# A routing phase that starts from the marked logits instead of from its predecessor's token indices

## The chip, the cores and the metric

The kernel runs on one core of one Trainium2 chip. The metric is the device time of one execution in microseconds (us). The core has five engines that work side by side: TensorE (PE, with its weight loads shown apart as PEld), VectorE (DVE), ScalarE (ACT), GpSimd (POOL) and SyncE (SP), which here only issues transfers. Each takes its instructions strictly in the order in which the program lists them.

## What is computed

Three layers follow one another (shapes: batch 8, 8 heads, 576 positions, 64 channels, so 4608 tokens of 512 channels; 8 experts with a hidden width of 1024; a last hidden width of 2048):

```python
x = linear_attention(q, k, v)
logits = x @ w_gate
order = argsort(-logits.flatten())
for idx in order:
    tok, e = idx // 8, idx % 8
    if assigned[tok] >= 0 or counts[e] >= 576: continue
    assigned[tok] = e; counts[e] += 1
for e in range(8):
    mask = assigned == e
    out[mask] = relu(x[mask] @ w1[e]) @ w2[e]
h = out @ w_in
return (h * clip(h + 3, 0, 6) / 6) @ w_out
```

The greedy assignment gives every expert exactly 576 tokens. Whichever expert fills up first can be settled without the others, and its tokens with it; what is left is the same problem with one expert fewer.

## The kernel before

**Routing.** `phase(ph)` (from L804) settles one expert. It takes the largest logit of each token (`m`, L808), marks which expert it belongs to (`eq`, `oh`), and finds the cut of each expert by eight rounds of counting (`counts`, `digit`): one comparison on VectorE (`ge`, L766), a product on TensorE (L777), two small VectorE steps with another product between them (`blk` L780, L785, `cnt` L788), then `hit` (L795) and one more product (L798) whose result the next round needs. So a round goes back and forth between the two engines three times. The expert that fills up first is `ei` (L889); its tokens are marked in `sel` (L874). From `sel` two things follow. One is the list of token indices: five MAX (L896) and four match-and-replace steps (L901), a comparison of 640 columns (`ind`, L894 and L898), ten small products (L911), three steps on `eq5`, and at last `gi` (L920). The other is that the settled expert and tokens are struck out of the logits `L` (L927, L928), from which the next phase reads.

**Experts.** `gather(ph)` fetches the 576 tokens in five tiles by an indirect transfer from POOL (`xg`, L1000), scales them on VectorE (L1006), transposes them on TensorE (L1019, four blocks a tile) and splits each result into a high part on ScalarE (L1024) and a low part on VectorE (L1029), both in `xT`, of which there is one buffer. `expert(ph)` does two halves of 288 tokens. Each half has 96 products with w1 (L1049, called A here) and 96 with w2 (L1071, called B); the eight results of A in each half are `h` (L1053, L1058). `xT` is free again after A of the second half. `load_expert(ph)` reads `ei` and loads 16 weight chunks of 256 KB (`st`, L980 and L983), each of which ScalarE (L497) and VectorE (L954) split into two parts.

**What sets the order.** The program lists its operations with their inputs and outputs, and a planner (`Sched`) places them by a list schedule: each engine takes, in planned time, the ready operation of highest priority. Routing phases after the first have a priority just above that of the expert products. The planned order of each engine is then the program's order. So routing phase ph + 1 stands between the products of expert ph, on TensorE and on VectorE, and what an edit does to a dependency shows as another order of all engines.

The calls at the end stand like this, and the first phase has nothing of an expert beside it, only the end of the attention layer:

```python
phase(0); gather(0); load_expert(0)
for ph in range(E):
    if ph + 1 < E: phase(ph + 1)
    expert(ph)
    if ph + 1 < E: load_expert(ph + 1); gather(ph + 1)
```

After the experts, the last layer (L1231, L1259) takes more than half of the time. Its weights are converted (`conv`, L1079 and on) from the time on at which the gather of phase 6 is done.

Of the kernel before, what the change touches and what calls it, by code (L numbers as in the profile page):

```python
# [15 lines left out]
OP = mybir.AluOpType  # L16
AX = mybir.AxisListType
# [29 lines left out]
class Sched:  # L47
# [17 lines left out]
    def op(self, eng, dur, fn, r=(), w=(), prio=0, lat=None, pen=None, u=()):  # L65
        i = len(self.ops)
        deps = set()
        for n in r:
            deps.update(self.writers.get(n, ()))
            self.readers.setdefault(n, []).append(i)  # L70
        for n in w:
            if any(x != i for x in self.readers.get(n, ())):
                deps.update(x for x in self.readers[n] if x != i)
                self.writers[n] = []
                self.readers[n] = [i] if n in r else []
            if n in self.bufof and n not in self.first:
                self.first[n] = i
                deps.update(self.writers.get(("pool", self.bufof[n][3]), ()))
            self.writers.setdefault(n, []).append(i)
        for n in set(r) | set(w) | set(u):  # L80
            if n in self.bufof:
                self.users.setdefault(n, []).append(i)
        if isinstance(eng, str):
            eng = [(eng, dur)]
        self.ops.append((eng, fn, deps, prio + self.base, lat, pen or dict(PENALTY)))
        return i
# [127 lines left out]
def tile_attn_moe_mlp(ctx, tc, q, k, v, w_gate, w1, w2, w_in, w_out, out):  # L214
    nc = tc.nc
    V, S, P, T, Y = nc.vector, nc.scalar, nc.gpsimd, nc.tensor, nc.sync
# [14 lines left out]
    def dve(n, x=1, ps=False):  # L231
        return ((130 if ps else 64) + n / x) / 0.96
# [12 lines left out]
    op = sc.op  # L245
# [24 lines left out]
    def const(name, shape, dt=F32):  # L270
        return (main if name in ("idxf", "idx", "spacer", "three") else PL["route"][1]).tile(shape, dt, name=name)
# [44 lines left out]
    L = const("L", [128, NCOL, E])  # L316
# [372 lines left out]
    m = const("m", [128, NCOL])  # L689
# [45 lines left out]
    n288 = NCOL * E  # L735
# [4 lines left out]
    def vop(n, f, r, w, x=1):  # L740
        op("dve", dve(n, x), f, r=r, w=w, prio=prio[0], lat=None if prio[0] == -1 else SLACK.get(w[0]))
# [62 lines left out]
    def phase(ph):  # L804
        odd = ph % 2
        last = ph == E - 1
        gate = [("gi", ph - 1)] if ph else []
        vop(n288, lambda e: V.tensor_reduce(m, L, axis=AX.X, op=OP.max), ["L"] + gate, ["m"])  # L808
        if not last:
            vop(n288, lambda e: V.tensor_tensor(eq, L, per_c(m), op=OP.is_equal), ["L", "m"], ["eq"])  # L810
            vop(NCOL, lambda e: V.tensor_scalar(ks, m.bitcast(I32), 31, 0x7FFFFFFF, op0=OP.arith_shift_right,
# [321 lines left out]

    prio[0] = -1
    phase(0)
    prio[0] = RPR
    gather(0)
    load_expert(0)
    for ph in range(E):
        if ph + 1 < E:  # L1140
            phase(ph + 1)
        expert(ph)
        if ph + 1 < E:
            load_expert(ph + 1)
            gather(ph + 1)
# [191 lines left out]
```

## Time and profile before

| | |
|---|---|
| median of 3 runs | 1499.53 us (1495.55 to 1502.17) |
| the profiled execution | 1508.03 us, its span 1505.6 us |
| PE busy | 1412.7 us, 94% |
| PEld, DVE, ACT, POOL busy | 1229.8, 673.0, 444.0, 600.4 us |
| mean granted clock of PE | 0.971 of full speed |

The profiled execution is 8.5 us above the median; differences are worked out inside it and then taken off the median. "PE busy" counts any time in which a product is under way, whatever the clock is, so a stretch can be fully busy and yet do less than another. The clock column gives the mean of the granted TensorE clock as a share of 2.4 GHz; its other level is 1.2 GHz, so 0.75 over a stretch is half of it at each.

### The profile page before, as it was taken

What the parts mean: (1) busy time and instruction counts of PE and PEld (TensorE: products, weight loads), DVE (VectorE), ACT (ScalarE), POOL (GpSimd) and SP (SyncE); (2) the same over time, 40 slices, a digit from 0 to 9 for tenths busy, and PEclk for the clock granted to TensorE, in tenths of its full rate; (3) what the DMA queues carried; (4) which work ended last, traced back from release to release, by engine and by line L of the source; (5) the groups of instructions that cost most, each with busy time, mean ns of one, the idle gap of its engine ahead of it and who ended that gap; (6) DMA issues with size and microseconds to landing.
All of it is one profiled execution on the core that took longest, in us unless ns stands there. A gap on an engine that the chain in (4) does not pass through costs nothing.

```text
span 1505.6 us, 23079 instructions
## 1 busy us (share of the span) xinstructions
PE 1412.7 (94%) x8738; PEld 1229.8 (82%) x8738; DVE 673.0 (45%) x1646; ACT 444.0 (29%) x858; POOL 600.4 (40%) x752
## 2 busy tenths in 40 slices
PE   5889599989999998899999999999999999999997
PEld 4778598989889898799788888888888888888886
DVE  7996668676675867875761111111111111111110
ACT  3656334233242434454432121211212121121111
POOL 6784301010110105755675353543535353353433
PEclk9999788999999999999999999999999999999999
DMA  9683535133250438767411010100101010010000
GB/s 317 206 251 112 185 104 164 59 117 103 82 172 32 150 92 264 221 217 252 134 61 57 1 56 1 43 14 1 57 0 56 1 51 6 0 43 0 29 1 28
DMA packets 130559, 140.76 MB, mean 93 GB/s; under 512 B 21264, under 2 KB 104208, under 8 KB 130448
## 3 DMA queue, kind: packets, MB, share of 16 engines
q1 hardware_dynamic: 124496, 119.73, 25.4%
q0 software_dynamic: 5952, 19.56, 3.7%
q8 instruction: 68, 1.11, 0.3%
q14 instruction: 43, 0.35, 0.1%
HBM read 104.51 MB, written 34.75 MB: 92 GB/s over the span
## 4 chain that ended last, share of the span: by engine, by line
PE 70%; DVE 12%; DMA 9%; issue 3%; POOL 3%; ACT 2%; SPq 0%; POOLq 0%; DVEq 0%; ACTq 0%
PE acc L1259 24%; PE mm L1231 23%; PE mm L1071 8%; PE mm L1049 8%; DMA st<-in_moe_w_dram 5%; PE px L619 2%; DMA wh<-co 2%; DVE m L384 1%; PE pkv L520 1%; DVE wq L954 1%; DVE xg L1006 1%; POOL out_dram L1277 1%; PE tr L1019 1%; DMA cs<-in_moe_w_in_dram 1%; DMA ys<-yd 1%
## 5 line engine op out<-in xcount | busy, mean ns | idle before, releaser
L1237 DVE SCALAR_TENSOR_TENSOR t<-t,mm 128x512 f32<-128x512 f32 x144 | 98.8, 687 | 540.2 <-ACT t L1236 530.6
L1236 ACT ACTIVATE t<-mm,three 128x512 f32<-128x512 f32 x144 | 99.1, 689 | 557.8 <-PE mm L1231 544.4
L501 POOL TENSOR_SCALAR G<-t 128x512 fp32r<-128x512 f32 x124 | 78.2, 631 | 365.7 <-DVE t L1237 362.6
L1259 PE MATMUL acc<-wq,G 128*128 128x512 f32 x864 | 211.9, 393 | 3.5 <-ACT G L497 1.6
L1231 PE MATMUL mm<-yT,wq 128*128 128x512 f32 x864 | 207.2, 389 | 0.0
L1259 PEld LDWEIGHTS acc<-wq,G 128*128 128x128 f32 x864 | 162.4, 189 | 41.7 <-POOL G L954 5.3
L1231 PEld LDWEIGHTS mm<-yT,wq 128*128 128x128 f32 x864 | 162.1, 188 | 33.6
L1000 POOL DMA_INDIRECT xg<-xd,gi x40 | 46.8, 1171 | 352.8 <-issue 307.1
L954 POOL TENSOR_TENSOR G<-t,G 128x512 fp32r<-128x512 f32 x139 | 179.4, 1291 | 12.1 <-ACT G L497 1.6
L1071 PE MATMUL mm<-h,wq 128*128 128x288 f32 x960 | 143.9, 306 | 0.0
L1049 PE MATMUL mm<-xT,wq 128*128 128x288 f32 x960 | 141.4, 304 | 0.0
L1071 PEld LDWEIGHTS mm<-h,wq 128*128 128x128 f32 x960 | 134.7, 195 | 2.4 <-issue 2.4
L1049 PEld LDWEIGHTS mm<-xT,wq 128*128 128x128 f32 x960 | 132.8, 192 | 0.8 <-DVE h L1058 0.3
L1231 PE MATMUL mm<-yT,w 128*128 128x512 f32 x432 | 103.4, 389 | 0.0
L1231 PEld LDWEIGHTS mm<-yT,w 128*128 128x128 f32 x432 | 81.1, 188 | 16.8
L1259 PE MATMUL acc<-w,G 128*128 128x512 f32 x384 | 92.3, 389 | 0.0
L1259 PEld LDWEIGHTS acc<-w,G 128*128 128x128 f32 x384 | 72.0, 188 | 15.1 <-POOL G L954 0.2
L1053 ACT ACTIVATE h<-mm 128x288 fp32r<-128x288 f32 x128 | 51.1, 405 | 84.5 <-PE mm L1049 46.9
L1058 DVE SCALAR_TENSOR_TENSOR h<-mm,h 128x288 fp32r<-128x288 f32 x128 | 57.4, 450 | 15.7 <-ACT h L1053 15.0
L497 ACT ACTIVATE wq<-st 128x512 fp32r<-128x512 f32 x78 | 48.9, 630 | 43.7 <-DMA st<-in_moe_w_dram 43.1
L1117 POOL TENSOR_TENSOR ca<-ct,cl 128x256 int32<-128x256 int32 x64 | 50.1, 787 | 27.2 <-DVE ct L1113 18.4
L954 DVE TENSOR_TENSOR wq<-st,wq 128x512 fp32r<-128x512 f32 x76 | 51.9, 685 | 14.4 <-ACT wq L497 13.4
(241 smaller groups left out, 2193.5 us busy)
## 6 DMA issues: line engine op xcount, KB each, us to landing
st<-in_moe_w_dram SPq DMA_DIRECT2D x124, 256.0 KB
yd<-yo SPq DMA_DIRECT2D x64, 144.0 KB
xd<-xs SPq DMA_DIRECT2D x32, 260.0 KB
lk<-in_k_dram SPq DMA_DIRECT2D x16, 512.0 KB
wu<-in_v_dram SPq DMA_DIRECT2D x16, 512.0 KB
wl<-in_q_dram SPq DMA_DIRECT2D x16, 512.0 KB
cs<-in_moe_w_in_dram SPq DMA_DIRECT2D x32, 256.0 KB
cs<-in_moe_w_out_dram SPq DMA_DIRECT2D x32, 256.0 KB
```

The costliest lines, as they stand in the source:

```text
L497: S.activation(o, i, AF.Copy)
L501: P.tensor_scalar(o, i, 1.0, 0.0, op0=OP.mult, op1=OP.add)
L954: EN[e].tensor_tensor(t[:, 1], view(X[src]), t[:, 0].bitcast(F32), op=OP.subtract)
L1049: T.matmul(p[:, :HC], w[:, a, k_], X[XT][:, b_, k_, o:o + HC], start=(k_ == 0 and (a, b_) == (0, 0)), stop=(k_ == 3 and (a, b_) == (1, 0)))
L1053: op("act", act(HC), lambda e, pk=pk, hn=hn: S.activation(hn()[:, 0], X[pk][:, :HC], AF.Relu), r=[pk], w=[hk, (hk, 0)])
L1058: V.scalar_tensor_tensor(t[:, 1], X[pk][:, :HC], 0.0, t[:, 0].bitcast(F32), op0=OP.max, op1=OP.subtract)
L1071: T.matmul(p[:, :HC], w[:, a, 128 * d:128 * d + 128], h[:, b_], start=(f_ == 0 and (a, b_) == (0, 0)), stop=(f_ == NFE - 1 and (a, b_) == ...
L1117: op("pool", pool(256), lambda e: P.tensor_tensor(X[A].bitcast(I32), X[T_], X[L_], op=OP.add), r=[T_, L_, A], w=[A], prio=CVP)
L1231: T.matmul(p, w[:, a, d], X[YT][:, b_, d], start=(d == 0 and (a, b_) == (0, 0)), stop=(d == 3 and (a, b_) == (1, 0)))
L1236: op("act", act(512), lambda e: S.activation(tn(), X[pk], AF.Relu, bias=three), r=[pk], w=[tk])
L1237: op("dve", dve(512, ps=True), lambda e: V.scalar_tensor_tensor(X[tk], X[tk], 6.0, X[pk], op0=OP.min, op1=OP.mult), r=[pk, tk], w=[tk])
L1259: T.matmul(p, g[:, a, 128 * t:128 * t + 128], w[:, b_], start=(f_ == 0 and (a, b_) == (0, 0)), stop=(f_ == NFM - 1 and (a, b_) == (1, 0)))
```

## The change

`phase(ph)` for ph > 0 no longer names `gi` of phase ph - 1 as an input of its first operation. The logits `L`, with the last expert and its tokens struck out, remain its input.

```diff
     def phase(ph):
         odd = ph % 2
         last = ph == E - 1
-        gate = [("gi", ph - 1)] if ph else []
-        vop(n288, lambda e: V.tensor_reduce(m, L, axis=AX.X, op=OP.max), ["L"] + gate, ["m"])
+        vop(n288, lambda e: V.tensor_reduce(m, L, axis=AX.X, op=OP.max), ["L"], ["m"])
```

One line is gone, so line numbers from L808 on are one lower in the changed program. The arithmetic is the same; the planner orders all of it anew. Two places show it.

VectorE, where phase 0 ends and phase 1 begins. `idw`, `gi` and `idxf` are the end of phase 0's indices, `m`, `eq`, `ks` the start of phase 1. Before:

```order
L918 TENSOR_REDUCE idw<-eq_236 128x5
L920 TENSOR_SCALAR gi<-idw 128x5
L922 TENSOR_TENSOR idxf<-idxf,idw 128x5
L808 TENSOR_REDUCE m<-L 128x36
L810 TENSOR_TENSOR eq<-L,m 128x288
L811 TENSOR_SCALAR ks<-m 128x36
L813 TENSOR_TENSOR eq<-eq,wfirst 128x288
```

With the change, right after the second MAX of phase 0:

```order
L807 TENSOR_REDUCE m<-L 128x36
L897 SCALAR_TENSOR_TENSOR ind<-iota,off_230,ind 128x640
L900 MATCH_REPLACE score<-ids,score 128x36
L809 TENSOR_TENSOR eq<-L,m 128x288
L895 MAX ids<-score 128x8
L810 TENSOR_SCALAR ks<-m 128x36
```

and where `gi` of phase 0 now stands:

```order
L914 TENSOR_TENSOR eq_236<-iota,kk 128x200
L780 TENSOR_TENSOR blk<-rt,colm 128x64
L916 TENSOR_TENSOR eq_236<-eq_236,rt 128x200
L917 TENSOR_REDUCE idw<-eq_236 128x5
L919 TENSOR_SCALAR gi<-idw 128x5
L921 TENSOR_TENSOR idxf<-idxf,idw 128x5
```

Twelve instructions of phase 1, from `m` to the `blk` of its first round, now stand ahead of `gi` of phase 0, between its steps.

TensorE, where expert 0 ends and expert 1 begins: `tr` is a transpose of gathered tokens, `mm<-h` is B of expert 0, `mm<-xT` is A of expert 1, `rt` belongs to routing. Before, the first transposes stand behind the last of B:

```order
L1071 MATMUL mm<-h,wq 128x288 x12
L785 LDWEIGHTS samen
L785 MATMUL rt<-blk,samen 128x64
L1071 MATMUL mm<-h,wq 128x288 x6
L798 LDWEIGHTS ones_110
L798 MATMUL rt<-sat,ones_110 128x1
L1019 MATMUL tr<-ident,xg 128x64 x4
```

and, after five products L777 of a routing round, the rest of them just ahead of A:

```order
L777 MATMUL rt<-oh,ge 128x64
L1019 MATMUL tr<-ident,xg 128x128 x12
L785 LDWEIGHTS samen
L785 MATMUL rt<-blk,samen 128x64
L1049 MATMUL mm<-xT,wq 128x288 x6
```

With the change the first transposes stand 36 products ahead of the end of B:

```order
L1070 MATMUL mm<-h,wq 128x288 x12
L1018 MATMUL tr<-ident,xg 128x64 x4
L785 LDWEIGHTS samen
L785 MATMUL rt<-blk,samen 128x64
L1070 MATMUL mm<-h,wq 128x288 x6
L1018 MATMUL tr<-ident,xg 128x128 x4
```

and B and A meet without a transpose between them:

```order
L777 LDWEIGHTS ge
L777 MATMUL rt<-oh,ge 128x64
L1070 MATMUL mm<-h,wq 128x288 x6
L1048 MATMUL mm<-xT,wq 128x288 x6
L785 LDWEIGHTS samen
L785 MATMUL rt<-blk,samen 128x64
```

At each of the later boundaries the transposes have likewise moved from the last dozen of B, or from behind it, into B or ahead of it. Counted in the 16 steps `h` that each expert has on VectorE, `gi` of phases 1 to 6 stood behind `h` number 16, 32, 47, 64, 80 and 95, and stands behind number 14, 27, 40, 56, 72 and 88; `ei` stood behind 10, 24, 40, 56, 72 and 88 and stands behind 8, 24, 40, 54, 68 and 82. The order of the products of the last layer is the same.

## Rows read from the trace of the kernel before

**Rows 1.** The page: busy tenths and granted clock of PE, 40 slices.
```profile
PE   5889599989999998899999999999999999999997
...
PEclk9999788999999999999999999999999999999999
```

**Rows 2.** Stretches: length, busy PE, PEld, DVE, ACT, POOL, granted clock, DMA share, GB/s.
```profile
245.00:265.00 20.00, 16.52 (x104) 14.43 (x103) 14.06 (x35) 6.70 (x14) 3.08 (x3) 0.74 0.40 139
300.00:330.00 30.00, 24.46 (x180) 23.19 (x179) 21.95 (x57) 12.04 (x23) 5.14 (x5) 0.89 0.50 155
368.00:394.00 26.00, 22.27 (x176) 20.62 (x176) 21.67 (x58) 11.32 (x22) 7.08 (x5) 1.00 0.60 185
432.00:456.00 24.00, 20.42 (x153) 18.77 (x153) 19.97 (x53) 11.63 (x23) 6.09 (x5) 0.94 0.60 189
500.00:528.00 28.00, 24.87 (x190) 23.20 (x189) 21.49 (x57) 11.35 (x23) 6.76 (x5) 0.94 0.40 127
557.00:586.00 29.00, 22.34 (x167) 21.16 (x166) 25.83 (x69) 14.75 (x29) 11.09 (x10) 0.94 0.77 235
262.00:300.00 38.00, 38.00 (x310) 36.49 (x308) 23.31 (x95) 9.69 (x22) 0.00 (x0) 1.00 0.17 53
394.00:432.00 38.00, 38.00 (x310) 36.56 (x309) 23.88 (x95) 9.71 (x23) 0.00 (x0) 1.00 0.18 56
```

**Rows 3.** Waits of PE, 240 to 586 us: total us, times, longest us.
```profile
PE rt L785 <- DVE blk L780: 8.3, 5, 3.8
PE tr L1019 <- DVE xT L1029: 4.4, 4, 2.3
PE rt L911 <- DVE ids L903: 3.7, 3, 2.0
PE rt L911 <- DVE ids L904: 2.6, 5, 1.2
PE tr L1019 <- DVE xg L1006: 2.4, 5, 0.7
```

**Rows 4.** Waits of PE, 586 to 705 us.
```profile
PE tr L1019 <- DVE xT L1029: 3.9, 1, 3.9
PE tr L1019 <- issue: 3.5, 2, 2.3
```

**Rows 5.** Timeline of DVE, end of phase 0: start us, us, line, operation.
```profile
173.49 0.19 DVE L896 MAX8 ids<-score 128x8 f32<-128x36 f32 x1
...
179.70 0.32 DVE L920 TENSOR_SCALAR gi<-idw 128x5 int32<-128x5 f32 x1
...
180.01 0.44 DVE L808 TENSOR_REDUCE m<-L 128x36 f32<-128x288 f32 x1
...
182.64 0.76 DVE L766 SCALAR_TENSOR_TENSOR ge<-ra,iota 128x576 bf16<-128x576 f32 x1
183.95 0.23 DVE L780 TENSOR_TENSOR blk<-rt,colm 128x64 f16<-128x64 f32 x1 [0.54 <-PE rt L777]
```

**Rows 6.** The same at the end of phase 1.
```profile
231.23 0.19 DVE L896 MAX8 ids<-score 128x8 f32<-128x36 f32 x1
...
240.50 0.17 DVE L920 TENSOR_SCALAR gi<-idw 128x5 int32<-128x5 f32 x1
...
240.65 0.44 DVE L808 TENSOR_REDUCE m<-L 128x36 f32<-128x288 f32 x1
```

**Rows 7.** Line L920, 440 to 500 us: durations in ns, first and last start.
```profile
L920 DVE TENSOR_SCALAR gi<-idw x1: 158/158/158, 499.7 to 499.7; 128x5 int32<-128x5 f32 x1
```

**Rows 8.** Timelines of ACT, DVE, PE: one wait for weights, passed on.
```profile
315.64 0.63 ACT L497 ACTIVATE wq<-st 128x512 fp32r<-128x512 f32 x1 [4.20 <-DMA st<-in_moe_w_dram]
...
316.30 0.69 DVE L954 TENSOR_TENSOR wq<-st,wq 128x512 fp32r<-128x512 f32 x1 [3.60 <-ACT wq L497]
...
317.18 0.21 PE L785 MATMUL rt<-blk,samen 128*128 128x64 f16 x1 [3.83 <-DVE blk L780]
```

**Rows 9.** Timeline of PE: a group of four transposes at full clock.
```profile
325.84 0.66 PE L1019 MATMUL tr<-ident,xg 128*128 128x128 f32 x4 [0.80 <-DVE xT L1029]
```

## The prediction

> **What bounds the kernel now.** I read the page's slices first [rows 1]. A slice is 37.6 us. From the 18th on (640 us, the last expert and the last layer) PE has a 9 in every slice, at full clock, so nothing is to be had there but from an earlier start. A 5, and clocks of 7 and 8, stand in slices 5 to 7, where the attention layer gives way to the experts; an 8 stands in slices 16 and 17, near the end of the experts; between them a 9 hides short stops. So the next view is the busy time in stretches [rows 2]: the first six hold one boundary between two experts each, the last two lie inside an expert. Inside, PE is busy for 38.00 of 38 us at full clock and does 310 products. At each boundary it is busy for less than the stretch, and the clock is lower in five of the six. The two undisturbed stretches give 76 us / 620 = 0.1226 us a product, with routing among them. The six boundary stretches last 157 us together and hold 970 products, which at that rate are 118.9 us. About 100 of these are transposes (20 for each expert, some of the first stand ahead of the stretch or behind it); a group of four takes 0.66 us [rows 9], 0.165 each, which adds some 4.2 us. So **33.9 us** of the 157 are lost. PE is idle for 157 - 130.9 = 26.1 us of them; the other 7.8 us I put down to products at the lower clock.
>
> What it waits for stands in the list of waits [rows 3]. The transposes and the ten products of the index list wait for DVE; the largest entry, 8.3 us, is a routing product waiting for `blk`, and behind that is another thing: ScalarE waited 4.20 us for a weight chunk, DVE stood 3.60 us behind it, and PE 3.83 us behind `blk`, which is next in DVE's queue [rows 8].
>
> Why are the transposes late? Because the indices are. Phase by phase `gi` comes at 179.70 [rows 5], then 240.50 [rows 6], and that of phase 5 at 499.7 [rows 7]: (499.7 - 179.7) / 5 = 64.0 us a phase. The next phase's `m` starts 0.15 us behind `gi` at 240.65, though the logits were struck out before the second MAX at 231.23. PE's own work in that time, counted in the code: 384 products and 20 transposes of an expert, and 69 products of a routing phase (eight rounds of five L777 and one L785, seven L798, and 14 behind them). 473 x 0.1226 = 58.0 us, and the transposes' 20 x 0.042 on top make it 58.8. So the loop **routing, indices, next routing** (64.0) is longer than PE's work for an expert (58.8), and PE waits for the difference at each boundary.
>
> **The change, part by part.**
>
> *The wait that goes.* From phase 1 on, `m` can start after the second MAX: 240.65 - 231.23 = 9.4 us earlier against its own `gi`. The twelve instructions that now stand among the index steps put `gi` back. Their cost is read where they stand alone: from `m` at 180.01 to the end of the first `ge` at 182.64 + 0.76 = 183.40 is 3.4 us, and `blk` adds at most 0.23 [rows 5]. The new loop would be 64.0 - 9.4 + 3.4 = 58.0 us, just under PE's 58.8. So the routing loop stops being what is late, by a little, and **PE's own queue is late next**, with what else holds it up.
>
> *The first phase.* Here the same twelve instructions are pure loss, since PE and everyone else wait for `gi` of phase 0: nothing of an expert covers them. The lower bound is 0, if they fit into DVE's gaps; the only gap of size is the wait for the index products, about half a microsecond as in the `blk` row. The upper bound is 3.6. I take **+3.4 us**, the row itself. The gathers, the first multiplies and expert 0 follow by as much.
>
> *The boundaries.* The gathers, issued from POOL once `gi` is there, move ahead with it; POOL has nothing else to do in these stretches (0.00 busy in the undisturbed ones, [rows 2]), so they pass no other work on their queue. On TensorE the transposes now stand inside B, with products behind them that cover ScalarE's and DVE's splits. What PE loses to late indices and transposes should go; what it loses to `blk` behind the weights I leave in full, as the loads are the same ones, started by `ei`, which has moved by nothing to six steps. So of 26.1 us idle, 8.3 stay and **17.8 go**. Of the gather of the last phase, the 3.5 us for which two transposes were not yet there [rows 4] go too, as its `gi` now stands seven or eight steps earlier; the 3.9 us for `xT` I leave, since there DVE is behind with the conversion of the last layer's weights.
>
> *The clock.* At the first boundary the granted clock is 0.74 over 20 us [rows 2]: about 10 us at 1.2 GHz. At the third it is 1.00, with 3.7 us idle of 26, so stops don't always bring it down, nor would fewer stops bring all of it back. I let half of the 7.8 us return: **3.9**. The Trainium skill, "TensorE: Matmul & The Clock Gate", section "What's actually happening", has it that the low clock is the default and that activity lifts it; by that rule alone the whole 7.8 would return once the stops are gone, and the sum would be 3.9 us lower. The stretches agree with it in part: no stretch without a stop has a lower clock, and one with stops has none either.
>
> *SP's queue.* The reading of `ei` stands at the same place or a few stores earlier in it, with no new wait ahead. I cost it at nothing; the stores of expert results cover it, which nobody waits for until the last layer.
>
> *The last layer.* Its weights are converted after the gather of phase 6, and both move ahead together with the experts; its products stand in the same order. Nothing.
>
> Sum: 17.8 + 3.9 + 3.5 = 25.2 us gained, 3.4 lost, **21.8 us** less. From the profiled 1508.0 that is 1486.2; its execution is 8.5 us above the median, so from the median of 1499.5 I predict **1478 us**. Its own range: with 0 to 3.6 for the first phase, nothing or all of the clock, and a quarter of the 17.8 staying, 1470 to 1486.
>
> **The rivals.**
>
> *All of it goes.* With the routing ahead by more at each phase, the weights too are asked for earlier (`ei` moves by up to six steps), and the waits behind them vanish as well. Then 33.9 + 3.5 + 3.9 - 3.4 = 37.9 us less: **1462**. For it: the lead of `gi` grows from phase to phase, in the order, from 2 to 8 steps. Against: 58.0 and 58.8 are close, so on the chip that lead can be had only slowly.
>
> *The wait moves.* DVE remains as full: at the fourth boundary it is busy for 19.97 of 24 us [rows 2], and now two phases share its queue. If only the waits go that name the index list and the gathered tokens (3.7 + 2.6 + 2.4 = 8.7, [rows 3]), and the rest comes back as waits for `blk` and `h` inside B, the gain is 8.7 - 3.4 = 5.3: **1494**, no change that a measurement of this kernel can tell (about 0.5%, 7.5 us).
>
> *Slower: the gathers fall into the weight loads.* Before, `ei` starts 16 loads and the gathers come when a good part of these has landed. Now the gathers come a few steps behind `ei`. Each boundary could then have the stop of 3.83 us [rows 8] which so far one has in full: six of them are 23.0 instead of 8.3, 14.7 more. If half of the 17.8 then stays as well, because a DVE that waits for weights holds up `xT` too, the sum is +14.7 + 3.4 - 8.9 = +9.2: **1509**. It is slower by more than 7.5 us from the point at which the added stops exceed 7.5 - 3.4 + 8.9 = 13.0 us, 2.2 a boundary. For it: the chain through ScalarE, DVE and PE is there, and it began while gathers ran. Against: the loads are not needed so soon; A of the next expert comes a whole B later, and only the fixed order of the queues makes a late chunk hurt. The Trainium skill, "DMA: Bandwidth & Descriptors", section "Issuing engines are not separate DMA queues", says that transfers from SyncE and GpSimd run on the same 16 engines and interleave. That is the rule that speaks against this change; that a chunk was late just while gathers were out agrees with it, no more.
>
> **How the numbers follow.** Forecast 0.62, all of it 0.15, moved wait 0.14, slower 0.09. The two-loop sum, 58.0 against 58.8, carries the forecast; that the two are so close keeps its chance from being higher. The range takes in the forecast, the full gain with 5 us below it for the runs' own spread, and the moved wait up to a gain of nothing: 1457 to 1501. Faster by over 0.5% (below 1492): 0.62 + 0.15 = 0.77. Within 0.5%: 0.14. Slower: 0.09.
>
> **What would show it.** Right: `gi` of phase 0 near 183; a mean distance of `gi` of 58 to 61 us over phases 0 to 5; transposes that start without a wait, inside B; the list of waits without the index rows, with `blk` still there; clock 1.00 at most boundaries; expert 7 ending some 20 us earlier and the last layer as long as before. Wrong: a distance of `gi` still at 64 (the moved wait), or waits of ScalarE for weights grown at every boundary with `blk` behind them (slower), or no idle left at all (all of it).

## The result, and the profile after

The changed kernel takes 1486.94 us (1486.37 to 1487.82, 5 runs) beside 1502.17 us for the kernel before (1495.55 to 1503.77, 5 runs): a ratio of 0.9909, 95% interval 0.9886 to 0.9931. On another chip it was 1489.95 beside 1505.28, ratio 0.9902 (0.9882 to 0.9921). So some 15 us are gained. The profiled execution has a span of 1485.3 us, 20.3 less than before.

First the slices of the page of the changed kernel, against [rows 1]:

```profile
PE   5889689999999998899999999999999999999997
...
PEclk9999879999999999999999999999999999999999
```

The 8 of PE in slice 9, where expert 1 gives way to expert 2, is a 9 now, and from slice 7 on the clock has a 9 in every slice; the 8s in slices 16 and 17 have stayed. The larger view is the busy time in three long stretches: experts 0 to 5, experts 6 and 7, the last layer. Columns as in [rows 2]. The kernel before:

```profile
191.00:584.00 393.00, 366.53 (x2837) 347.39 (x2835) 277.11 (x909) 138.04 (x286) 41.48 (x34) 0.96 0.37 114
584.00:705.00 121.00, 112.28 (x799) 110.88 (x798) 87.89 (x172) 58.46 (x156) 78.90 (x107) 0.94 0.70 223
705.00:1505.00 800.00, 788.08 (x3454) 647.83 (x3452) 154.54 (x225) 152.86 (x260) 365.42 (x417) 1.00 0.10 35
```

The changed kernel:

```profile
197.00:565.00 368.00, 354.90 (x2843) 338.09 (x2842) 280.93 (x923) 141.70 (x303) 50.06 (x47) 0.99 0.43 133
565.00:683.00 118.00, 108.03 (x785) 105.23 (x784) 76.71 (x156) 53.36 (x145) 63.26 (x88) 0.99 0.68 219
683.00:1485.00 802.00, 787.86 (x3456) 646.95 (x3454) 154.16 (x229) 151.31 (x257) 360.28 (x416) 1.00 0.09 31
```

Three things stand in the first line of each. The stretch is 25.0 us shorter for nearly the same products (2837 and 2843). PE's idle time in it has halved, from 26.5 to 13.1 us. And PE's *busy* time has fallen by 11.6 us, because the mean clock rose from 0.96 to 0.99: fewer products run at 1.2 GHz. In the second line the idle time has not fallen (8.7 and 10.0 us). The busy time has, by 4.2 us: some 2 us of it are eleven transposes, which now stand ahead of the stretch, and most of the rest is clock (0.94 and 0.99). The last layer is the same within 2 us, and everything begins 6 us later.

The start of each expert, read from PE's timeline as its first product with `xT`, gives the account (us):

| | expert 0 | 1 | 2 | 3 | 4 | 5 | 6 | 7 | end of 7 | span |
|---|---|---|---|---|---|---|---|---|---|---|
| before | 191.1 | 257.7 | 326.4 | 390.7 | 454.0 | 518.1 | 584.0 | 652.6 | 704.5 | 1505.6 |
| changed | 197.5 | 263.1 | 322.9 | 384.5 | 442.9 | 503.8 | 564.6 | 628.5 | 682.9 | 1485.3 |

Start +6.4, six experts -25.8, experts 6 and 7 -2.2, last layer +1.3: -20.3. Of the +6.4, 1.8 lie ahead of anything that the change moves (`sel` of phase 0 starts at 173.6 instead of 171.8).

The loop that the prediction rests on, against [rows 5] and [rows 7]; line L919 is `gi`, of phase 0 and of phase 5:

```profile
L919 DVE TENSOR_SCALAR gi<-idw x1: 171/171/171, 185.7 to 185.7; 128x5 int32<-128x5 f32 x1
...
L919 DVE TENSOR_SCALAR gi<-idw x1: 158/158/158, 465.2 to 465.2; 128x5 int32<-128x5 f32 x1
```

(465.2 - 185.7) / 5 = 55.9 us a phase instead of 64.0, while the experts start (564.6 - 197.5) / 6 = 61.2 us apart instead of 65.5. So `gi` runs ahead: it comes 11.8 us before expert 0 starts and 38.6 us before expert 5 does (11.4 and 18.4 before). PE's timeline where expert 0 ends and expert 1 begins, with L1070 for B and L1048 for A:

```profile
255.69 0.46 PE L1018 MATMUL tr<-ident,xg 64*128 64x64 f32 x4
...
256.12 1.03 PE L1070 MATMUL mm<-h,wq 128*128 128x288 f32 x6
257.80 0.66 PE L1018 MATMUL tr<-ident,xg 128*128 128x128 f32 x4 [0.65 <-DVE xg L1005]
258.21 1.03 PE L1070 MATMUL mm<-h,wq 128*128 128x288 f32 x6
...
262.24 1.05 PE L1070 MATMUL mm<-h,wq 128*128 128x288 f32 x6
263.12 0.96 PE L1048 MATMUL mm<-xT,wq 128*128 128x288 f32 x6
```

The transposes stand among B, and A follows B without a stop. A group of four takes 0.66 us; the clock is 1.00 from 250 to 266 us. What PE still waits for from 197 to 565 us, against [rows 3]:

```profile
PE mm L1048 <- DVE h L1057: 3.4, 2, 1.9
PE rt L798 <- DVE hit L795: 2.7, 3, 1.3
PE tr L1018 <- issue: 2.2, 1, 2.2
PE rt L785 <- DVE blk L780: 1.5, 2, 1.2
PE tr L1018 <- DVE xg L1005: 1.4, 2, 0.7
PE rt L777 <- DVE ge L766: 1.0, 1, 1.0
PE tr L1018 <- DVE xT L1028: 0.5, 1, 0.5
PE rt L910 <- DVE ids L902: 0.2, 1, 0.2
```

The index list (`ids`) has gone from 6.3 to 0.2 us and `blk`, which I had left in full, from 8.3 to 1.5. The waits for `h` are new. Those for `hit` have grown; the kernel before had this row from 191 to 584 us:

```profile
PE rt L798 <- DVE hit L795: 1.6, 2, 1.0
```

### The profile page after: what moved, and what is told of

Read it like the earlier page. It is cut to its first block, busy times and chain, and to the rows that moved or that the text cites. A ratio compares the mean times of both kernels' runs of the same rounds, so it can differ in the third digit from the quotient of the medians.

```text
span 1485.3 us, 23045 instructions
## 1 busy us (share of the span) xinstructions
PE 1397.5 (94%) x8738; PEld 1213.6 (82%) x8738; DVE 669.7 (45%) x1654; ACT 441.2 (30%) x859; POOL 589.7 (40%) x743
## 4 chain that ended last, share of the span: by engine, by line
PE 67%; DVE 12%; DMA 9%; POOL 5%; issue 3%; SPq 2%; ACT 2%; POOLq 0%; ACTq 0%; DVEq 0%
PE acc L1258 23%; PE mm L1230 22%; PE mm L1048 9%; PE mm L1070 7%; DMA st<-in_moe_w_dram 3%; PE px L619 2%; DMA cs<-in_moe_w_in_dram 1%; DMA cs<-in_moe_w_out_dram 1%; POOL out_dram L1276 1%; SPq L358 1%; DVE wq L953 1%; DMA ys<-yd 1%; POOL G L953 1%; PE pkv L520 1%; DVE ct L1112 1%
## 5 line engine op out<-in xcount | busy, mean ns | idle before, releaser
L953 POOL TENSOR_TENSOR G<-t,G 128x512 fp32r<-128x512 f32 x137 | 176.3, 1287 | 11.6 <-ACT G L497 1.3
L1070 PE MATMUL mm<-h,wq 128*128 128x288 f32 x960 | 141.6, 303 | 2.8 <-DVE h L1057 1.9
L1048 PE MATMUL mm<-xT,wq 128*128 128x288 f32 x960 | 138.8, 299 | 1.5 <-DVE h L1057 1.5
L1070 PEld LDWEIGHTS mm<-h,wq 128*128 128x128 f32 x960 | 131.5, 191 | 3.7 <-DVE h L1057 2.3
L1048 PEld LDWEIGHTS mm<-xT,wq 128*128 128x128 f32 x960 | 130.1, 188 | 3.1 <-DVE h L1057 1.7
L1258 PEld LDWEIGHTS acc<-w,G 128*128 128x128 f32 x384 | 72.1, 188 | 14.9
L953 DVE TENSOR_TENSOR wq<-st,wq 128x512 fp32r<-128x512 f32 x77 | 58.1, 764 | 10.2 <-ACT wq L497 10.1
```

Of the source, the lines that this page charges most:

```text
L953: EN[e].tensor_tensor(t[:, 1], view(X[src]), t[:, 0].bitcast(F32), op=OP.subtract)
L1048: T.matmul(p[:, :HC], w[:, a, k_], X[XT][:, b_, k_, o:o + HC], start=(k_ == 0 and (a, b_) == (0, 0)), stop=(k_ == 3 and (a, b_) == (1, 0)))
L1070: T.matmul(p[:, :HC], w[:, a, 128 * d:128 * d + 128], h[:, b_], start=(f_ == 0 and (a, b_) == (0, 0)), stop=(f_ == NFE - 1 and (a, b_) == ...
L1258: T.matmul(p, g[:, a, 128 * t:128 * t + 128], w[:, b_], start=(f_ == 0 and (a, b_) == (0, 0)), stop=(f_ == NFM - 1 and (a, b_) == (1, 0)))
```

## The experiments

The theory on trial is that of two loops: routing, indices and the next routing on one side, PE's own work for an expert on the other; the longer sets the pace. Every edit lets the planner order all engines anew, so earlier indices and the new places of the transposes go together, and no run parts them. "The changed kernel's second measurement" below is the following run. The last three runs were taken on another chip than the rest, so times are compared by their ratio to the kernel before on the same chip.

> The changed kernel once more, beside the others on one chip. 1487 us, expert 0 starting near 197 us, gi of phase 0 about 12 us behind its sel (7.9 before), the starts of the experts 61.2 us apart on average.

1489.95 us, ratio 0.9902 (0.9882 to 0.9921). Expert 0 starts at 197.8, expert 6 at 570.3: 62.1 us apart. Between its profiled execution and the first measurement's, a single expert of this same kernel differs by up to 3 us (expert 4 takes 63.2 and 60.9 us, expert 6 60.9 and 63.9), so a difference of that size in one expert says little.

**The wait back in phase 1 alone.**

```diff
-        gate = [("gi", ph - 1)] if ph else []
+        gate = [("gi", 0)] if ph == 1 else []
```

> The wait is put back for phase 1 alone. Theory of the two loops: phase 0's index list is free again of phase 1's instructions, gi of phase 0 comes 7.9 us behind sel instead of 12.1, expert 0 starts 4 to 5 us sooner; phase 1 begins later by 4.6 us against sel, which its later lead over the experts absorbs, so nothing is lost behind it: 1482 to 1484 us. Rival (the lead of the first phase is what all later phases live on, since the routing loop still paces): the first boundary is late as before, 4 to 5 us are lost again, and the time stays at 1486 to 1488.

1489.85 us, ratio 0.9898 (0.9880 to 0.9917): no gain over the 1489.95 of the changed kernel, as the rival had it; the expected 1482 to 1484 us did not come. Expert 0 does start 3.6 us sooner (194.2), but expert 1 at 261.6 instead of 262.0. The reason stands in `gi` of phase 1, first of this run, then of the changed kernel's second measurement:

```profile
L920 DVE TENSOR_SCALAR gi<-idw x1: 169/169/169, 242.3 to 242.3; 128x5 int32<-128x5 f32 x1
```

```profile
L919 DVE TENSOR_SCALAR gi<-idw x1: 167/167/167, 242.0 to 242.0; 128x5 int32<-128x5 f32 x1
```

It comes at the same time. What phase 0's indices lose to phase 1 is what phase 1 wins, and expert 1 starts by phase 1's indices: 19.3 us behind this `gi` here, 20.0 in the changed kernel. At this boundary the routing is not yet ahead, as the rival said. So the cost in phase 0 is real where it stands, and no part of the time at the end.

**The wait taken away in phase 1 alone.**

```diff
-        gate = [("gi", ph - 1)] if ph else []
+        gate = [("gi", ph - 1)] if ph > 1 else []
```

> The wait is taken away for phase 1 alone and stays for phases 2 to 7. Two loops: phase 0 loses its 4 to 5 us, the first boundary gains about as much, and from there each phase takes 64 us again, so the experts start 65 us apart and the time is that of the kernel before, 1499 to 1504. Rival (any overlap near the start is enough, the gain is a single shift): the gain of the change remains for the most part, below 1494.

1505.56 us, ratio 1.0002 (0.9985 to 1.0020): the time of the kernel before (1505.28 on this chip), as the two loops have it, though above the 1499 to 1504 that stood for it. `gi` from phase 0 to 5,

```profile
L920 DVE TENSOR_SCALAR gi<-idw x1: 172/172/172, 186.1 to 186.1; 128x5 int32<-128x5 f32 x1
...
L920 DVE TENSOR_SCALAR gi<-idw x1: 158/158/158, 498.4 to 498.4; 128x5 int32<-128x5 f32 x1
```

is 62.5 us a phase, 63.4 after the first, and the experts are (580.4 - 197.9) / 6 = 63.8 us apart. One early start is used up at once; the gain needs it at every phase.

**The wait back from phase 3 on, and from phase 5 on.**

```diff
-        gate = [("gi", ph - 1)] if ph else []
+        gate = [("gi", ph - 1)] if ph >= 3 else []
```

> The wait is put back from phase 3 on (phases 1 and 2 stay free). Two loops: the lead at phase 3 is small (gi of phase 2 stands 23.5 us ahead of its expert, of which some 19 are needed for the gathers and transposes), and a loop of 64 us loses 3 to 5 us on the experts at each phase, so after one or two phases the experts are 64 us apart again: 1493 to 1500 us, between the kernel with phase 1 alone free (1505.6) and the one with the wait from phase 5 on (1484.2). Rival (a lead once won carries to the end): 1484 to 1490.

1496.14 us, ratio 0.9938 (0.9916 to 0.9960): in the range of the theory. The experts are 61.7 us apart up to expert 3 and 63.9 from there to expert 6. The 63.9 is no even step: experts 3, 4 and 5 take 60.2, 62.9 and 68.5 us. What shows the pace is the lead of `gi`: experts 3 to 6 start 18.6, 18.0, 18.4 and 21.8 us behind their `gi`, as in the kernel before (17.2 to 21.8), where the changed kernel has 31.9 to 41.3. So the lead is used up at expert 3 already, and from there the indices decide again when an expert starts.

> The wait is put back for phases 5, 6 and 7 alone. Two loops: in the changed kernel gi of phase 5 is 39 us ahead of the start of its predecessor's expert by then plus a period, so the routing has slack to wait three times for its own indices (about 9 us each) without an expert noticing: 1485 to 1489 us, at most 2 us from the changed kernel. Rival (every boundary pays by its own wait): three boundaries lose 4.3 us each again, 1498 to 1501.

(The same edit with `ph >= 5`.) 1484.22 us, ratio 0.9868 (0.9844 to 0.9892). The lead of the routing suffices for three waits, so the rival falls; but the time is better than the theory's range and 5.7 us better than the changed kernel. Their executions do not overlap (1481.4 to 1487.8 us, and 1489.0 to 1491.1). The stretches of experts 4, 5 and 6 show where:

```profile
444.50:501.90 57.40, 57.40 (x470) 55.47 (x468) 42.98 (x142) 21.32 (x45) 5.48 (x5) 1.00 0.41 118
501.90:558.90 57.00, 56.52 (x452) 54.97 (x452) 43.75 (x145) 24.43 (x53) 15.18 (x15) 1.00 0.61 188
558.90:627.30 68.40, 58.60 (x405) 57.59 (x405) 53.91 (x91) 33.70 (x88) 48.63 (x61) 0.90 0.74 238
```

Expert 4 takes 57.4 us with PE busy in all of it, at full clock: that is PE's own work with a routing phase, 1.4 us under the 58.8 that I had counted. Expert 6 takes 68.5, with 9.8 us idle and a clock of 0.90. So two things are left: short stops in experts 4 and 5 of the changed kernel (63.2 and 63.4 us in its second measurement, 60.9 and 60.8 in its first), and the stretch in which the last gather meets the conversion of the last layer's weights.

**A shorter index list instead.** The wait stays; the planner is told that the steps of the list follow without a gap (`lat=0`), so it puts nothing between them.

```diff
-        vop(NCOL, lambda e: V.tensor_tensor(score, sel, tok1, op=OP.mult), ["sel"], ["score"])
+        vop(NCOL, lambda e: V.tensor_tensor(score, sel, tok1, op=OP.mult), ["sel"], ["score"], lat=TL)
...
-            vop(NCOL, lambda e, i=i: V.max(ids[:, 8 * i:8 * i + 8], score), ["score"], ["ids", ("ids", i)])
+            vop(NCOL, lambda e, i=i: V.max(ids[:, 8 * i:8 * i + 8], score), ["score"], ["ids", ("ids", i)], lat=TL)
```

(The same for the match-and-replace step, `off`, the first of `ids2`, `kk`, `eq5` and `idw`.)

> The wait stays in every phase, as before; instead the planner is told that the steps of the index list follow one another without a gap, so that nothing is put between them. Two loops: what counts is the length of the loop from routing over indices to the next routing, however it is shortened. The list falls from 12.8 us on average (sel to gi) to about 8, the loop from 64.0 to 59 or 60, and phase 0 loses nothing: experts 61 us apart, 1482 to 1488 us. Rival (what pays is that the next routing runs beside the index list): a third of the gain at most, 1494 to 1501.

1495.06 us, ratio 0.9924 (0.9900 to 0.9949): outside the theory's range and inside the rival's. The time alone would speak for the rival; the stretches don't. The theory's steps hold and its sum doesn't. `gi` of phases 0 and 5, then experts 0 to 5 and expert 6 as stretches:

```profile
L920 DVE TENSOR_SCALAR gi<-idw x1: 171/171/171, 182.6 to 182.6; 128x5 int32<-128x5 f32 x1
...
L920 DVE TENSOR_SCALAR gi<-idw x1: 172/172/172, 480.2 to 480.2; 128x5 int32<-128x5 f32 x1
```

```profile
196.10:570.90 374.80, 358.87 (x2842) 340.61 (x2841) 282.64 (x915) 133.72 (x283) 45.23 (x39) 0.99 0.40 118
570.90:638.90 68.00, 58.90 (x407) 57.23 (x406) 52.88 (x95) 35.55 (x91) 46.65 (x56) 0.92 0.80 256
```

The loop is 59.5 us as expected, and experts 0 to 5 take 374.8 us: 18.1 less than in the kernel before (392.9), and 2.3 and 7.6 more than in the two measurements of the changed kernel. So the loop's length does count, however it is shortened; a third of the gain at most, as the rival had it, is not what these experts show. But expert 6 takes 68.0 us instead of 60.9 or 63.9, much as in the kernel before (68.6) and with the wait from phase 5 on (68.5): I had left that stretch out of the sum.

> The same steps without gaps, and the wait taken away as in the change. Two loops: the next routing finds hardly a gap to begin in, so the order is nearly that of the run above, and so is the time, within 4 us of it: 1480 to 1488. Rival (the two edits add up): some 10 us below the better of the two, under 1477.

(The same edit without the wait.) 1494.17 us, ratio 0.9929 (0.9904 to 0.9954): within a microsecond of the run above, so the edits don't add up in the time. It is outside the range by the same stretch: experts 0 to 5 take 369.6 us, 5.2 less than above, and expert 6 takes 72.1, 4.1 more. What lengthens expert 6 in these two runs was not tried in them.

**The conversion later.**

```diff
-        op("dma", dma(128 * 2048), f, r=[("there", E - 2, 4)], w=[sk], prio=CVP)
+        op("dma", dma(128 * 2048), f, r=[("there", E - 1, 4)], w=[sk], prio=CVP)
```

> The changed kernel, with the conversion of the last layer's weights started only after the last tile of the last gather. Theory of the surplus with the wait from phase 5 on (5.7 us faster than the change): with a long lead the conversion begins inside expert 5 and its work on VectorE makes h late there; held back, experts 4 to 6 lose less, and the kernel gains 3 to 6 us if the last layer does not wait for its weights: 1484 to 1487. Rival (the routing's own rounds, crowded into experts 4 and 5, cost it): no gain, or a loss of several us, as the conversion then ends later: 1489 to 1500.

1487.70 us, ratio 0.9879 (0.9856 to 0.9903), an interval that overlaps the changed kernel's: inconclusive in the time. In the profile it is not: expert 5 takes 59.4 us (63.4), expert 6 56.6 (60.9), expert 7 56.5 (54.2), the last layer 805.8 (801.9). Experts 5 and 6 are 8.3 us shorter, and 6.2 of this come back in expert 7 and the last layer. Expert 6 is the safer of the two, as expert 5 took 60.8 us in the changed kernel's first measurement. Expert 4 is no case of the conversion at all: it takes 60.9 us here, as in that first measurement, and has ended before the conversion starts in any of these kernels (553 us and later). Its stops in the changed kernel's second measurement are waits in the routing's own rounds:

```profile
PE rt L798 <- DVE hit L795: 2.1, 1, 2.1
PE rt L777 <- DVE ge L766: 1.0, 1, 1.0
```

With the wait from phase 5 on, no such wait is left in expert 4. So the rival has that part of the surplus; what the conversion costs shows in expert 6, and in expert 5 at most in part.

> The wait from phase 5 on and the late conversion together. If the 68.5 us of expert 6 in the run with the wait from phase 5 on come from the conversion beside the last gather, that expert falls to 57 to 60 us and the last layer gives some 4 us back, as in the run with the late conversion: 1476 to 1481 us. Rival (expert 6 is long because gi of phase 7 is late, whatever the conversion does): 1484 to 1489.

1482.29 us, ratio 0.9841 (0.9816 to 0.9865): 1.3 us above the range, and no clear gain over the wait from phase 5 on alone (0.9844 to 0.9892). Expert 6 falls from 68.5 to 55.2 us, so it was the conversion and not the late `gi`, which stands where it stood. The last layer gives back 9 us (809.1 after 800.3), more than expected.

> The same, with the conversion started after the third of the last gather's five tiles instead of the last one. Same theory: expert 6 a few us longer than in the run beside it, the last layer a few us shorter, the sum within 3 us of it. Rival as there: 1484 to 1489.

(`("there", E - 1, 2)` with the wait from phase 5 on.) 1478.76 us (1476.64 to 1482.11), ratio 0.9817 (0.9794 to 0.9841): the fastest of all, ahead of both kernels, though its interval overlaps that of the run above. Expert 6 and the last layer:

```profile
560.80:620.40 59.60, 55.37 (x406) 54.46 (x405) 42.96 (x80) 29.81 (x77) 36.63 (x44) 0.97 0.71 224
676.90:1477.60 800.70, 787.98 (x3456) 646.99 (x3455) 154.79 (x233) 151.96 (x259) 359.99 (x418) 1.00 0.11 36
```

Expert 6 gives up 4.4 us of the last run's gain and the last layer pays nothing (800.7, and 800.3 with the wait from phase 5 on alone).

**Phase 0's index list without GpSimd beside it.**

```diff
-        op([("dve", dve(n))] if psum or quiet and not late else [("pool", pool(n))] if late else lo(n), 0, f,
+        op([("dve", dve(n))] if psum or quiet and not late else [("dve", dve(n))] if late else lo(n), 0, f,
```

> The changed kernel, with the low parts of expert 0's first four weight chunks split on VectorE instead of GpSimd, so that GpSimd has nothing to do while phase 1's first instructions run inside phase 0's index list. Theory (the two engines shut each other out): the four small instructions that took 0.8 to 1.1 us there (ks, key, k, ra) take 0.17 to 0.27 as elsewhere, and the stretch from sel to the first ge, 9.1 us, is 2.5 to 3.5 us shorter; gi does not come earlier by as much, since VectorE now has four splits of 0.68 us among its steps. Rival (the instructions are slow by themselves, or wait for a semaphore): they stay at 0.8 to 1.1.

The changed kernel: DVE's timeline inside the list, and POOL's at the same time.

```profile
177.15 1.13 DVE L810 TENSOR_SCALAR ks<-m 128x36 int32<-128x36 int32 x1
...
178.74 1.09 DVE L813 TENSOR_TENSOR key<-m,ks 128x36 int32<-128x36 int32 x1
179.75 0.44 DVE L814 TENSOR_REDUCE wm<-eq 128x36 f32<-128x288 f32 x1
...
180.21 0.82 DVE L815 TENSOR_SCALAR k<-key 128x36 int32<-128x36 int32 x1
...
181.49 1.07 DVE L817 TENSOR_SCALAR ra<-k 128x36 f32<-128x36 int32 x1
...
182.67 0.73 DVE L766 SCALAR_TENSOR_TENSOR ge<-ra,iota 128x576 bf16<-128x576 f32 x1
```

```profile
176.62 5.90 POOL L953 TENSOR_TENSOR wu<-wl,wu 128x512 fp32r<-128x512 f32 x4 [8.64 <-ACT wu L497]
```

With POOL idle, the same instructions in the same order:

```profile
177.50 0.17 DVE L810 TENSOR_SCALAR ks<-m 128x36 int32<-128x36 int32 x1
...
178.11 0.20 DVE L813 TENSOR_TENSOR key<-m,ks 128x36 int32<-128x36 int32 x1
...
178.68 0.17 DVE L815 TENSOR_SCALAR k<-key 128x36 int32<-128x36 int32 x1
...
179.29 0.19 DVE L817 TENSOR_SCALAR ra<-k 128x36 f32<-128x36 int32 x1
...
179.56 0.76 DVE L766 SCALAR_TENSOR_TENSOR ge<-ra,iota 128x576 bf16<-128x576 f32 x1
```

From `sel` (173.55 and 173.91) to the start of `ge` it is 9.1 us with POOL at work and 5.65 without, 3.5 less. `gi` comes 10.2 us behind `sel` instead of 12.1. A single execution took 1489.49 us (the kernel before 1504.01 on this chip), too little to tell a gain from none; as with the wait back in phase 1, none is seen.

## Why the prediction was right, point by point

The direction and the mechanism held, and the time of 1486.9 us lies in the range of 1457 to 1501, just outside the forecast's own 1470 to 1486. The gain was over-stated, 21.8 us against 15.2 between the medians. Two of the signs that were named missed: `gi` of phase 0 came at 185.7 instead of near 183, and the mean distance of `gi` is under the 58 to 61 us.

- *The two loops.* Right, and further than I had it: 55.9 us a phase instead of the 58.0 of the sum. The 3.4 us for the instructions that now stand among the index steps came out: from `m` to its `sel` it is 54.1 us on average in phases 1 to 5, 50.8 before. The 9.4 was too little: from `sel` to the next `m` it is 2.1 us instead of 13.4, so 11.3 are saved. I had read the 9.4 at the end of phase 1 alone, whose list is the shortest (11.2 us from `sel` to `gi`, 12.7 on average). With these instructions among its steps the list itself still fell to 10.8 us; why is not shown by a run. That PE is late next is shown: PE is busy for 354.9 of 368 us, and with a lead to spare an expert takes 57.4 us with no stop. The changed kernel's experts are still 61.2 us apart, so some stops are left.
- *The boundaries and the clock.* The sum of both terms was 21.7 and came out as 25.0; their split was wrong, and that the two errors nearly cancel is luck. Of the 17.8 us of idle only 13.4 went, as some stops moved to `h` and `hit`; of the clock I took half of 7.8, and 11.6 came back. Even the whole of the 7.8 was too little, since it counts the six boundary stretches alone, 157 of 393 us. At the same 0.1226 us a product and 0.042 more a transpose, the 2837 products of experts 0 to 5 are 352.9 us, and PE was busy for 366.5: 13.6 us too long, by this estimate, and 1.3 with the change. The Trainium skill's rule ("TensorE: Matmul & The Clock Gate", section "What's actually happening") is that activity lifts the clock; the 0.96 that became 0.99 when the idle time halved agrees with it. That no stretch without a stop has a lower clock, as I read it, holds for the stretches that I had looked at and not for the start of expert 0: from 191 to 198 us PE is busy throughout at 0.57, and had been busy for 9.6 of the 26 us before; from 198 us on it is 1.00. The change leaves that loss as it was: the first 53 us of expert 0 have 0.94 with it, as the first 54 us had without.
- *`blk` behind the weights stays in full.* Wrong: 8.3 became 1.5 us. The rule that the prediction set against the change did not show as a cost: over experts 0 to 5 ScalarE waits 54.3 us for weight chunks instead of 70.8, although the gathers came earlier. Why these waits shrank is not shown by a run; the rival "all of it goes" had named `ei`, which moved ahead too.
- *The first phase.* +3.4 us was +4.2 in `gi`. With POOL idle `gi` comes 10.2 us behind `sel` instead of 12.1, four splits of 0.7 us on VectorE included; so some 2 us are waits for POOL, which the sum did not have. The 7.9 us of the kernel before hold such waits too (the second step of `ids2`, L904, takes 1.20 us there beside POOL and 0.20 in the changed kernel), so what the instructions cost by themselves stays open. The step that failed is "pure loss": the run with the wait back in phase 1 wins those microseconds at expert 0 and has lost them at expert 1.
- *The last gather.* 3.5 us of waits for late transposes became 1.6, but PE is idle for as long as before in experts 6 and 7, more than half of it on `h`. The 2 us gained there are clock, and transposes done earlier.
- *The last layer.* +1.3 us instead of nothing.
- *Profile and median.* Here the sum as a whole went wrong. The profiled executions differ by 20.3 us in span, close to the 21.8; the medians by 15.2, and by 15.3 on the other chip. Of the 9.2 us by which the forecast missed, 1.5 lie between the sum and the profiled executions and 5.1 between these and the medians; the other 2.6 are the base, 1499.5 from three executions and 1502.2 from five. The profiled execution of before is at 1508.0, and the other runs of that kernel on all chips reach from 1495.5 to 1511.4; those of the changed kernel on its first chip reach from 1486.4 to 1487.8. I took a difference inside an execution 8.5 us above the median off that median; some of what the change removes was larger in that execution than in others. One such part can be named: the profiled execution has a mean granted clock of 0.971, and of the 39 other executions of that kernel for which it is on record none has less. The twelve of them above 1508 us have 0.973 on average, the seven under 1503 us 0.976. How much of the 5.1 us this is stays open, since only profiled executions have rows.

Of the rivals, "the wait moves" came true in part: stops for `h`, and longer ones for `hit`. "All of it goes" did in part too, with `blk` and the clock. The slower case did not occur.

## What to carry to other kernels

When an engine waits at every turn of a loop, first find out whether another loop through other engines is longer than its own work: the mean distance of one marked instruction over many turns (64.0 us of `gi`) against the work per turn (57.4 measured, 58.8 counted) says so, and says how much there is to gain before the other loop takes over. Once a dependency that only kept order is gone, look at what now meets: here keeping the wait in the last three phases and starting the conversion a little later was worth another 11 us or so (a ratio of 0.9817 instead of 0.9902). And a delay at the start counts only if the next turn waits for it.

## What had not been expected of the hardware

Four DVE instructions on 128 x 36 elements took 0.82 to 1.13 us while POOL ran a TENSOR_TENSOR on 128 x 512, and 0.17 to 0.20 when POOL was idle. They are TENSOR_SCALAR with input and output in SBUF, and TENSOR_TENSOR with both inputs there. The TENSOR_REDUCE among them (`wm`, 0.44) was not slowed, nor were the larger TENSOR_TENSORs that started right behind a held one (0.45). The last held instruction ends at 182.56 us, POOL's last at 182.52. POOL's four instructions took 5.90 us in all, 5.07 before. The Trainium skill, "SBUF — State Buffer", section "Who interferes with whom", says that VectorE shares a pair of ports with GpSimd, that these two forms can need it, that whichever comes second waits until the other has finished, and that a reduction does not take part; the rows agree with it. Beside such a neighbour each of the four small steps took five to seven times as long.
